# Four weight loads of a two-block recurrent attention kernel: their order, and the queue that issues them

## The chip, the cores and the metric

The kernel runs on one core of a Trainium2 chip. Its time is the device time of one execution in microseconds (us). The kernel before was run 11 times; the median counts.

## The reference

Four blocks follow each other on 2048 tokens of width 512: A, B, A, B. Each adds its output to a residual stream and works on a layer norm of it. Both A blocks share their weights, and so do both B blocks.

Block A is attention with a recurrent memory: 64 segments of 32 tokens, each behind 8 memory rows, with 32 heads of width 128. The first 8 output rows of a segment are the memory of the next, so that the segments form a chain:

```
for s in range(n_seg):
    h = jnp.concatenate([mem, xs], axis=1)
    q, k, v = h @ Wq, h @ Wk, h @ Wv          # 512 x (32 heads x 128)
    p = softmax(where(mask, q k^T * scale, -1e9))
    o = (p v) @ Wo
    mem = o[:, :M, :]; outs.append(o[:, M:, :])
```

Block B is linear attention over all tokens, 32 heads of width 16, with the weights wqkv and wo.

## The kernel before, in words

All weights of block A stay on the chip: `Wq_sb`, `Wk_sb`, `Wv_sb` and `Wo_sb`, 4 MB each. They are loaded once, at the start. The three projections of a block of 32 rows are matmuls at line 785 (`project`); each projection is made in two halves of 16 matmuls of 512 columns. Line 999 (`out_proj`) multiplies by Wo and needs all four parts of it. Line 1024 (`next_mem`) turns the new memory rows for the next segment.

Queries and keys are turned after projection (`turned`), either on TensorE (line 807) or by a DMA transpose issued from SyncE (line 798). "Left" blocks hold the last 8 tokens of four segments together; line 835 makes their scores. Line 876 makes the scores of a segment. Line 735 (`warm`) is 14 matmuls without use for the result, behind the first segment's memory attention.

The order on every engine is fixed at build time. Each piece of work is a node added with an estimated cost and, for transfers, an estimated latency `lat`; `schedule` deals the nodes out to engines by simulating these estimates. A node with a place (`P.at(step, name)`) gets the priority step x 13.5 plus an entry of the table `OFFSET`, lowest first among those that are ready (line 254). A node without a place gets the length of the path behind it. Then `finalize` turns dependences into waits on semaphores. The device executes each engine's list in order.

The loads: two come from SyncE, the first memory rows (line 644) and the first 128 tokens (line 646). Wq, Wk and Wv come from ScalarE (line 651). The offset of "ld4", -27049.20, places Wv ahead of Wq. Their estimated latencies are 13.2, 23.7 and 34.8. Wo is loaded in four parts of 1 MB from SyncE (line 656); parts 0 and 1 wait for Wk, parts 2 and 3 for Wv, by `after`. The load of block B's wqkv (line 658) follows on SyncE, and waits for the last part of Wo. Block B's wo is loaded by GpSimd (line 663) and waits for wqkv.

Of the kernel before, what the change touches and what calls it, by code (L numbers as in the profile page):

```python
# [22 lines left out]

PERIOD = 13.5
OFFSET = {
    "ld0": (-123.05,),
    "ld1": (-42.20,),
    "ld2": (6.75,),
    "ld3": (-61.40,),
    "ld4": (-27049.20,),  # L30
    "startF": (31.55,),
    "prepF": (60.65, -70.40, -52.45, 13.25, -87.60, -51.75, -71.05, 30.70, -58.30, 4.70, -58.20),
    "left0F": (-67.40, -16.05, 42.40, -9.10, 43.45, -14.00, -72.75, 13.95, -5.65, 15.60, -9.65, -120.75, 45.95,
# [103 lines left out]
class _Prog:  # L137
# [27 lines left out]
    def add(self, engs, fn, cost, reads=(), writes=(), tiles=(), dsem=None, urgent=False, mode="full",  # L165
            after=(), lat=0.0):
        nd = _Node()
        nd.mode = mode
        nd.lat = lat
        nd.key = None  # L170
        if self.place is not None:
            step, name = self.place
            nd.key = (step, name, self.count)
            self.count += 1
        nd.soft = set()
        nd.engs = (engs,) if isinstance(engs, str) else tuple(engs)
        nd.cost = cost if isinstance(cost, dict) else {e: cost for e in nd.engs}
        nd.fn = fn
        nd.sync = set(after)
        nd.order = set()  # L180
        nd.tiles = tuple(tiles)
        nd.dsem = dsem
        nd.urgent = urgent
        nd.eng = nd.start = nd.done = nd.know = None
        nd.sig = False
        nd.val = 0
        nd.waits = []
        nd.idx = len(self.nodes)
        if dsem is not None:
            self.dma_tot[dsem] = self.dma_tot.get(dsem, 0) + 16  # L190
            nd.dval = self.dma_tot[dsem]
        for key in reads:
            st = self.res.setdefault(key, [None, []])
            if st[0] is not None:
                nd.sync.add(st[0])
            st[1].append(nd)
        for key in writes:
            st = self.res.setdefault(key, [None, []])
            if st[0] is not None and st[0] is not nd:
                nd.sync.add(st[0])  # L200
            for r in st[1]:
                if r is not nd:
                    nd.sync.add(r)
            st[0] = nd
            st[1] = []
        for tl in nd.tiles:
            if tl.ops:
                p = tl.ops[-1]
                if p.engs == ("pe",) and nd.engs == ("pe",):
                    nd.order.add(p)  # L210
                else:
                    nd.sync.add(p)
            tl.ops.append(nd)
        self.nodes.append(nd)
        return nd
# [270 lines left out]
def bass_interleave_layers__memory_aug_recurrent_mem_tr__linear_attn_block__prompt_kernel(  # L486
    nc: bass.Bass,
    A_x: bass.AP,
    A_mem0: bass.AP,
    A_Wq: bass.AP,  # L490
    A_Wk: bass.AP,
    A_Wv: bass.AP,
    A_Wo: bass.AP,
    A_seg_len: bass.AP,
    B_x: bass.AP,
    B_wqkv: bass.AP,
    B_wo: bass.AP,
    out: bass.AP,
):
    _build_kernel(nc, A_x, A_mem0, A_Wq, A_Wk, A_Wv, A_Wo, A_seg_len, B_wqkv, B_wo, out)  # L500


def _build_kernel(nc, A_x, A_mem0, A_Wq, A_Wk, A_Wv, A_Wo, A_seg_len, B_wqkv, B_wo, out):
# [23 lines left out]
    def sb(name, shape, dt=BF16):  # L527
        return E(nc.sbuf_tensor(name, shape, dt))
# [4 lines left out]
    Wo_sb = sb("Wo_sb", [128, H, D])  # L533
# [78 lines left out]
    P = _Prog(nc, banks)  # L612
    add = P.add
# [33 lines left out]
    late = []  # L647
# [4 lines left out]
    wo_view = A_Wo.rearrange("h e d -> e h d")  # L652
    P.at()
    for i in range(4):
        hs = slice(8 * i, 8 * i + 8)
        add("sp", lambda s, hs=hs: s.dma_start(Wo_sb[:, hs, :], wo_view[:, hs, :]), 0.9, writes=[("Wo", i)],
                 dsem="dWo%d" % i, after=[late[1 + i // 2]], lat=(12.5, 14.5, 7.3, 9.8)[i])
    add("sp", lambda s: s.dma_start(wqkv_sb[:, :, :], B_wqkv.rearrange("(c p) f -> p c f", p=128)), 0.5,
        writes=["wqkv"], dsem="dwqkv", after=[P.nodes[-1]], lat=5.0)
    late.append(P.nodes[-1])  # L660
# [37 lines left out]
    for j in range(4):  # L698
        q = slice(32 * j, 32 * j + 32)
        d = j % 2  # L700
# [8 lines left out]
        writes=["selz"])  # L709
# [10 lines left out]
    def _m0(t, tl=tl):  # L720
        for c in range(4):
# [4 lines left out]
         writes=["memT0"])  # L726
# [610 lines left out]
```

## Time and profile before

| | |
|---|---|
| time, median of 11 runs | 1808.25 us (1803.25 to 1812.69) |
| time of the profiled execution | 1807.0 us |
| its span, from first to last instruction | 1804.8 us |
| TensorE matmuls busy | 1678.2 us, 93% |
| ScalarE busy | 1166.2 us, 65% |
| VectorE busy | 954.1 us, 53% |
| GpSimd busy | 326.0 us, 18% |
| granted TensorE clock, mean | 0.994 |
| time to landing of Wv, Wq, Wk, from issue | 13.7, 23.2, 33.7 us |
| time to landing of a part of Wo | 5.8 to 8.9 us, median 7.1 |

The profile is of one execution. In its lines PE is TensorE, PEld its weight loads, DVE VectorE, ACT ScalarE, POOL GpSimd, SP SyncE; a q behind the name means the engine's queue of instructions that issue or wait. L785 is line 785 of the kernel. `arena_sb` is one large buffer that holds nearly all working tiles, so a DMA from `arena_sb` to `arena_sb` is a transpose of line 798. A line of waits names who waited, for whom, how long in total, how often, and the longest.

### The profile page before, as it was taken

The numbers are of one execution on the slowest core, as the hardware profiler recorded it, in microseconds if no ns is written. First come the engines' busy times: TensorE is split into PE (matmuls) and PEld (weight loads), VectorE is DVE, ScalarE is ACT, GpSimd is POOL, SyncE is SP. The second block draws the span as 40 slices with busy tenths as digits, with TensorE's granted clock in tenths as the row PEclk, the third lists the DMA queues.
The fourth block names the chain that finished last, engine by engine and source line by source line (L and its number), as shares of the span: only waits on it lengthen the run. The fifth ranks groups of instructions, "written<-read, shape, count | busy, mean of one in ns | idle before, by whom it ended". The sixth has DMA issues, their size and how long they took to land.

```text
span 1804.8 us, 104738 instructions
## 1 busy us (share of the span) xinstructions
PE 1678.2 (93%) x48282; PEld 1141.6 (63%) x48407; DVE 954.1 (53%) x3216; ACT 1166.2 (65%) x3109; POOL 326.0 (18%) x660
## 2 busy tenths in 40 slices
PE   3899999999999999999789999999999999999996
PEld 1566666666666676676556666667666666666673
DVE  2355555555545555555544555555555555545557
ACT  2566666666666666666556677666666666667665
POOL 2012111211211121121101112222112222211211
PEclk9999999999999999999989999999999999999999
DMA  8412222222222222122111222212222212222223
GB/s 340 119 36 44 41 44 47 42 44 44 42 44 44 47 41 47 41 43 47 28 23 33 45 49 44 50 41 48 47 43 50 44 42 50 44 48 43 54 52 124
DMA packets 235080, 99.29 MB, mean 55 GB/s; under 512 B 213624, under 2 KB 228784, under 8 KB 233104
## 3 DMA queue, kind: packets, MB, share of 16 engines
q1 hardware_dynamic: 211312, 60.22, 17.6%
q0 software_dynamic: 21744, 19.78, 4.9%
q10 hardware_dynamic: 1584, 12.58, 1.7%
q8 instruction: 379, 6.21, 1.5%
q14 instruction: 61, 0.50, 0.1%
HBM read 29.63 MB, written 10.49 MB: 22 GB/s over the span
## 4 chain that ended last, share of the span: by engine, by line
PE 73%; DMA 15%; DVE 5%; ACT 3%; issue 2%; POOL 1%; ACTq 0%; DVEq 0%
PE pb L785 37%; PE pb L999 13%; DMA arena_sb<-arena_sb 12%; PE pb L971 4%; PE pb L876 3%; PE pb L1161 2%; PE pb L903 2%; PE pb L807 2%; DMA Wk_sb<-in_A_Wk_dram 2%; PE pb L1195 1%; DVE arena_sb L619 1%; ACT arena_sb L618 1%; PE pb L948 1%; PE pb L1024 1%; PE pb L917 1%
## 5 line engine op out<-in xcount | busy, mean ns | idle before, releaser
L618 ACT ACTIVATE arena_sb<-pb 128x512 bf16<-128x512 f32 (+5 forms) x1387 | 705.5, 511 | 333.9 <-PE pb L785 278.0
L634 POOL DMA_DIRECT2D dx_sb<-y_sb x504 | 253.2, 509 | 872.0 <-DVE y_sb L1035 494.9
L785 PE MATMUL pb<-Wv_sb,arena_sb 128*32 128x512 bf16 x5120 | 380.7, 380 | 0.0
L619 DVE COPY arena_sb<-pb 128x512 bf16<-128x512 bf16 (+2 forms) x365 | 131.3, 361 | 396.7 <-PE pb L807 382.4
L785 PE MATMUL pb<-Wq_sb,arena_sb 128*32 128x512 bf16 x5120 | 321.4, 382 | 10.2 <-DMA Wq_sb<-in_A_Wq_dram 9.8
L785 PE MATMUL pb<-Wk_sb,arena_sb 128*32 128x512 bf16 x5120 | 321.4, 381 | 3.8 <-DMA Wk_sb<-in_A_Wk_dram 2.7
L999 PE MATMUL pb<-Wo_sb,arena_sb 128*32 128x256 bf16 x10368 | 315.9, 273 | 6.1 <-DVE arena_sb L920 5.2
L999 PEld LDWEIGHTS pb<-Wo_sb,arena_sb 128*32 128x32 bf16 x10368 | 263.6, 97 | 28.8 <-DVE arena_sb L920 16.2
L785 PEld LDWEIGHTS pb<-Wq_sb,arena_sb 128*32 128x32 bf16 x5120 | 144.4, 97 | 129.8 <-DMA Wq_sb<-in_A_Wq_dram 10.1
L785 PEld LDWEIGHTS pb<-Wk_sb,arena_sb 128*32 128x32 bf16 x5120 | 136.5, 97 | 118.3 <-DVE arena_sb L619 10.2
L619 DVE CAST arena_sb<-pb 128x512 bf16<-128x512 f32 (+3 forms) x346 | 164.7, 477 | 71.6 <-PE pb L785 37.7
L619 DVE COPY arena_sb<-arena_sb 32x320 bf16<-32x320 bf16 (+1 forms) x677 | 150.1, 222 | 86.8 <-PE pb L876 68.4
L618 ACT ACTIVATE outW_sb<-pb 128x128 fp32r<-128x128 f32 x323 | 89.5, 277 | 123.0 <-PE pb L999 117.5
L876 PEld LDWEIGHTS pb<-arena_sb 128*32 128x32 bf16 x8128 | 109.4, 94 | 91.1 <-DMA arena_sb<-arena_sb 43.4
L876 PE MATMUL pb<-arena_sb 128*32 128x8 bf16 x8128 | 132.1, 174 | 35.2 <-DMA arena_sb<-arena_sb 30.6
L785 PEld LDWEIGHTS pb<-Wv_sb,arena_sb 128*32 128x32 bf16 x5120 | 122.7, 95 | 54.7 <-issue 1.5
L971 PE MATMUL pb<-arena_sb 128*128 128x128 bf16 x1024 | 145.1, 218 | 5.5 <-issue 2.7
L887 ACT ACTIVATE arena_sb<-pb 128x192 bf16<-128x192 f32 (+1 forms) x256 | 83.8, 328 | 97.8 <-PE pb L876 96.7
L972 PE MATMUL pb<-arena_sb 128*128 128x32 bf16 x1024 | 127.3, 178 | 0.0
L1035 DVE TENSOR_TENSOR y_sb<-pb,outW_sb 64x256 bf16<-64x256 f32 x158 | 65.8, 417 | 98.4 <-ACT outW_sb L618 95.0
L807 PEld LDWEIGHTS pb<-id_sb,arena_sb 128*32 128x32 bf16 x4352 | 84.5, 96 | 44.5 <-issue 8.1
L894 DVE TENSOR_TENSOR arena_sb<-arena_sb 128x128 bf16<-128x128 bf16 x504 | 90.0, 220 | 39.2 <-ACT arena_sb L887 38.3
(116 smaller groups left out, 2102.2 us busy)
## 6 DMA issues: line engine op xcount, KB each, us to landing
arena_sb<-arena_sb SPq DMA_TRANSPOSE x368, 2.8
Wv_sb<-in_A_Wv_dram ACTq DMA_DIRECT2D x1, 4096.0 KB, 13.7
Wq_sb<-in_A_Wq_dram ACTq DMA_DIRECT2D x1, 4096.0 KB, 23.2
Wk_sb<-in_A_Wk_dram ACTq DMA_DIRECT2D x1, 4096.0 KB, 33.7
Wo_sb<-in_A_Wo_dram SPq DMA_DIRECT2D x4, 1024.0 KB, 7.1
xs_scratch<-x_sb POOLq DMA_DIRECT2D x32, 128.0 KB, 2.1
pq_scratch<-arena_sb POOLq DMA_DIRECT2D x32, 128.0 KB, 2.0
dx_sb<-y_sb POOLq DMA_DIRECT2D x252, 12.0 KB, 2.0
```

Of the source, the lines that this page charges most:

```text
L618: return e.activation(o() if callable(o) else o, i() if callable(i) else i, ACTF.Copy)
L619: return e.tensor_copy(o() if callable(o) else o, i() if callable(i) else i)
L634: add(eng, lambda e: e.dma_start(o, i), 0.55 if eng == "pool" else 0.4, reads=reads, writes=writes, dsem="%s%d" % (kind, k), lat=lat + (0. ...
L785: r = pe.matmul(tl.f32()[32 * j:32 * j + 32, 0:512], blk[:, c, :], W[:, c, o:o + 512], start=(c == 0), stop=(c == 3), tile_position=(0, 32 ...
L807: r = pe.transpose(tt.bf16()[32 * j:32 * j + 32, 128 * i:128 * i + 128], img[:, k, o:o + 32], id_sb[:, :], tile_position=(0, 32 * j))
L876: r = pe.matmul(tl.f32()[32 * j:32 * j + 32, 48 * i + o:48 * i + o + n], kk[:, hh, j, :], qT[:, hh, j, 0:n], start=True, stop=True, tile_p ...
L887: add("act", lambda a: a.activation(PQ[:, r2, b, :, 0:nq], tl.f32()[:, 0:192].rearrange("p (i q) -> p i q", i=4)[:, :, 0:nq], ACTF.Exp, sc ...
L894: add("dve", lambda v, a=a: v.tensor_tensor(Pm[:, k, a, :].rearrange("p (i j x) -> p i j x", i=4, j=4), PQ[:, r2, b, :, 40 * a:40 * a + 8] ...
L971: pe.matmul(o, vimg[:, r2, e], Pbx[:, hh, :, 0:32], start=True, stop=False)
L972: return pe.matmul(o[:, :, 24:32], vleft[:, g2, e], Pbx[:, hh, :, 32:40], start=False, stop=True)
L999: r = pe.matmul(tl.f32()[32 * j:32 * j + 32, 0:256], oT[:, 4 * hh + n, :], Wo_sb[:, 8 * n + hh, 256 * d:256 * d + 256], start=(hh == 0 and ...
L1035: add("dve", lambda v: v.tensor_tensor(y_sb[0:64, k, :], tl.f32()[0:64, 0:256], outW[64:128, w, :].bitcast(F32), ALU.add), c_dve(256), rea ...
```

## The change

Queries, keys, values: the five offsets of the single loads become zero, so ScalarE issues Wq, Wk and Wv in this order. The four parts of Wo move from SyncE to ScalarE and follow there without a wait. The planner's estimates for Wo change with it: an issue cost of 0.5 in place of 0.9, and latencies of 36.5 to 44.6 from the issue. SyncE keeps the two first loads, the transposes and wqkv. Nothing else differs in the source; the planner deals the whole program out again.

```diff
 OFFSET = {
-    "ld0": (-123.05,),
-    "ld1": (-42.20,),
-    "ld2": (6.75,),
-    "ld3": (-61.40,),
-    "ld4": (-27049.20,),
+    "ld5": (0.00, 10.00, 20.00, 30.00),
+    "ld0": (0.00,),
+    "ld1": (0.00,),
+    "ld2": (0.00,),
+    "ld3": (0.00,),
+    "ld4": (0.00,),
...
     P.at()
     for i in range(4):
         hs = slice(8 * i, 8 * i + 8)
-        add("sp", lambda s, hs=hs: s.dma_start(Wo_sb[:, hs, :], wo_view[:, hs, :]), 0.9, writes=[("Wo", i)],
-                 dsem="dWo%d" % i, after=[late[1 + i // 2]], lat=(12.5, 14.5, 7.3, 9.8)[i])
+        P.at(-6000, "ld5")
+        P.count = i
+        add("act", lambda a, hs=hs: a.dma_start(Wo_sb[:, hs, :], wo_view[:, hs, :]), 0.5, writes=[("Wo", i)],
+            dsem="dWo%d" % i, lat=36.5 + 2.7 * i)
+    P.at()
     add("sp", lambda s: s.dma_start(wqkv_sb[:, :, :], B_wqkv.rearrange("(c p) f -> p c f", p=128)), 0.5,
         writes=["wqkv"], dsem="dwqkv", after=[P.nodes[-1]], lat=5.0)
```

## The prediction

> **What bounds the kernel now.** I read the page first, then the chain of waits, then what TensorE waited for in the first 60 us and after it, then the queues of ScalarE and SyncE in order of time, then stretches. TensorE is busy 93% of the span, but not evenly (stretches; columns: us, then busy us of TensorE, its weight loads, VectorE, ScalarE, GpSimd, then clock, DMA share, GB/s):
> ```profile
> 0.00:60.00 60.00, 30.27 (x632) 16.46 (x636) 15.70 (x43) 17.96 (x48) 10.69 (x45) 0.97 0.86 311
> 60.00:850.00 790.00, 755.27 (x22346) 520.75 (x22382) 422.08 (x1461) 519.73 (x1400) 142.84 (x279) 1.00 0.24 44
> ```
> Half of the first 60 us is idle; afterwards TensorE works 96% of the time. The chain that ended last says how it starts:
> ```profile
> 1.83 33.74 DMA Wk_sb<-in_A_Wk_dram
> 35.57 0.04 issue
> 35.62 4.45 PE pb L785 x48
> ...
> 52.88 5.58 DMA arena_sb<-arena_sb
> 58.46 0.14 issue
> 58.60 0.28 PE pb L835 x16
> 58.87 0.87 PE pb L785 x16
> 59.74 1.77 PE pb L999 x64
> ```
> The key weights' landing at 35.57 starts it; from there to the first output projection (L999) is 59.74 - 35.57 = 24.2 us. Of TensorE's waits in these 60 us (total, times, longest) I show those that come after the first weights could be used; the 10.6 us at L760 above them pass before 14 us, while tokens and weights are still on their way:
> ```profile
> PE pb L785 <- DMA Wq_sb<-in_A_Wq_dram: 9.8, 1, 9.8
> PE pb L785 <- DMA Wk_sb<-in_A_Wk_dram: 2.7, 1, 2.7
> ...
> PE pb L835 <- issue: 1.9, 1, 1.9
> PE pb L835 <- DMA arena_sb<-arena_sb: 1.6, 1, 1.6
> ```
> The loads leave ScalarE as values, queries, keys, one behind the other, while TensorE uses them as queries, keys, values: the first use of Wv stands at 49.6, 35 us after it landed (0.80 + 13.7 = 14.5). Wo leaves SyncE in two pairs:
> ```profile
> 0.80 0.42 ACTq L651 DMA_DIRECT2D Wv_sb<-in_A_Wv_dram  x1
> 1.25 0.55 ACTq L651 DMA_DIRECT2D Wq_sb<-in_A_Wq_dram  x1
> 1.83 0.53 ACTq L651 DMA_DIRECT2D Wk_sb<-in_A_Wk_dram  x1
> 2.39 1.28 ACT L666 ACT_TABLE_LOAD   x1 [2.39 <-issue]
> ```
> ```profile
> 35.59 1.02 SPq L656 DMA_DIRECT2D Wo_sb<-in_A_Wo_dram  x2
> 43.42 4.83 SPq L798 DMA_TRANSPOSE arena_sb<-arena_sb  x2
> 48.30 1.21 SPq L656 DMA_DIRECT2D Wo_sb<-in_A_Wo_dram  x2
> 52.88 1.19 SPq L798 DMA_TRANSPOSE arena_sb<-arena_sb  x1
> ```
> The second pair waits for Wv, long there, but stands behind two transposes that need key work, so it leaves at 48.30 and lands at about 57 (5.8 to 8.9 us to landing). The DMA engines fall idle meanwhile (share 0.00 at 47 to 48 us).
>
> **What the Trainium skill says.** "DMA: Bandwidth & Descriptors", section "Issuing engines are not separate DMA queues": whichever engine issues a transfer, it runs on the same 16 DMA engines. So moving Wo to ScalarE adds no bandwidth; it takes away waits. The same page, "Queues, rings and completion order": an engine of the DMA works through one queue's ring in order and alternates between queues packet by packet. The trace agrees: three loads of one queue land at 14.5, 24.45 and 35.57, one after the other, and a transpose of SyncE's queue beside bulk traffic took 5.58 us against a median of 2.5 in the first 110 us. "TensorE: Matmul & The Clock Gate", Part 1: the array starts at half clock after an idle window of about 3.4 us. Here the stretch 36 to 39 us shows clock 0.50, after a gap of 2.7 us.
>
> **The change, part by part.**
> *Order of three loads.* Each is 4.19 MB and they follow each other at about 10 us. Queries land at 14.5 instead of 24.45, keys at 24.45 instead of 35.57 (11.1 us sooner), values at about 35.5 instead of 14.5. Query work took 24.51 to 32.95, 8.4 us, so it now ends at 22.9 and TensorE waits some 1.5 us for the keys. ScalarE's copies for the first token block end at 14.02, just before.
> *From keys to the first L999.* The same instructions take 23.9 us (35.62 to 59.56, its first start), stalls of 1.9 and 1.6 and the half clock included: 24.45 + 23.9 = 48.4. The values are first used at 49.6 - 11.1 = 38.5, 3 us after they land: hidden. Without that cover, each us late is one us.
> *Wo in the same queue.* Four more issues on ScalarE, at 0.42 to 0.55 each (L651; 0.40 to 0.59 on SyncE): about 2.0 us. Behind them stand the table load (2.39 to 3.67) and two small copies, which end at 4.1 and now at 6.1; the next work of ScalarE is at 10.90, behind the token load, so this is hidden with 4.8 us over. SyncE loses four issues (2.2 us) and two waits, so its transposes are no longer queued behind Wo.
> *When Wo lands.* Its rows are 1 KB. In the stretches 39 to 43 us the first pair moved at 384, 355, 355, 368 GB/s; 4.19 MB at 365 is 11.5 us. Data of the third weight fell off at about 33.5; four transposes now lie in this time. SyncE's queue took 17.6% of 1804.8 us for 368 transposes and some other loads, so at most 0.86 each: 3.5 us. Last comes landing after data, 1 to 2 us (Wk: 33.5 against 35.57). 33.5 + 3.5 + 11.5 + 1.5 = 50.0. All four parts are needed by the first L999, so Wo ends 1.6 us after TensorE's own 48.4 and sets it: 59.6 becomes 50.0, **9.6 us sooner**. Bounds: 48.4 with transposes that take little (11 us gain); 53 with transposes slowed and Wo at the 325 GB/s of 51 to 52 us (6.5 us gain).
> *What follows.* The wqkv load still waits for Wo's last part, then GpSimd's load of the second Wo: they move along (54.29 and 62.63 become about 50 and 58). The next transposes, 4.9 us after L999, meet them as they did before (4.17 us to landing at 64.47); I take 0.6 us for a worse meeting, from none to 1.4 (5.58 - 4.17). Nothing later hangs on a fixed time. The work after is bound by TensorE, so the head start should reach the end: 9.6 - 0.6 = **9.0 us**.
> *The order by the planner.* It deals all instructions out by its own figures, and these change a little, which I follow for order only. By the code, it takes queries to land at 14.1, keys 25.0, values 35.3, last Wo 46.96; now 13.7, 24.6, 36.1, 47.56. Thus it had already planned for queries, keys, values, and the order on TensorE should hardly alter: shifts of -0.4 to +0.8, and after the first L999 all work hangs on that one chain. I cost a different order at nothing, within -3 to +20 us.
>
> Sum on the profiled execution: span 1804.8 - 9.0 = 1795.8; its time is 1807.0 (2.2 us lie around the span), so 1798.0. The median, 1808.25, stands 1.25 above that execution: 1799.3.
>
> **The rivals.**
> *Eaten by new waits (no change).* Transposes at about 23 and 33 us now meet rows of 8 KB instead of 1 KB, alternating by packet. For: 5.58 us even beside small rows, and 1.9 us of unexplained issue at 43.65 with the DMA engines full, which may repeat. Against: those transposes are needed only at 45 to 47 us. It would take three stalls of about 3 us: 1808.
> *The planner deals otherwise (slower).* Place: the waits of TensorE on transposes, 30.6 us in 48 waits after 60 us, and idle in steady stretches of 4%. With 127 segments after the first, 0.15 us more in each is 19 us, less 9.0 is +10: 1818. It decides from 9.0 / 127 = 0.07 us a segment. For: shifts of 0.4 to 0.8 us that aren't equal let ready times cross, and priorities fitted one by one needn't suit another order. Against: the planned landings differ so little.
> *ScalarE held by its own queue (slower).* Wo adds 4096 rows of 1 KB to 1536 of 8 KB outstanding; if the queue can't hold them, ScalarE stands still at the issue. Held until t instead of 10.90, query work starts 3.6 later, then 8.4 and 23.9: first L999 at t + 36. It loses from t = 24; held until Wv is in (35), 1820. Against: no issue shown took over 0.59 us, though no more than three loads were ever queued here.
>
> **How the numbers follow.** A measurement tells this kernel from no change beyond about 0.2% (3.6 us). Head start carried: 0.57, its own range 1796 to 1802.5 (gain 12 to 6). Partly carried, 1802.5 to 1804.6: 0.04. Eaten: 0.13, 1804.6 to 1811.9. Planner: 0.20, mostly 1812 to 1828. ScalarE held: 0.06, 1812 to 1822. So faster 0.61, same 0.13, slower 0.26. The range for 8 in 10 leaves out little below and 0.15 above: 1795 to 1821.
>
> **What would show it.** Right: TensorE's wait for Wq nearly gone, one of 1 to 2 us for Wk, first L999 at 50 and released by Wo's landing, the last L999 (1767.8 at most now) some 9 us sooner, stretches after it still at 96%. Wrong in a step: a ScalarE issue of several us; a wait of L785 on Wv; L835 waiting on transposes for longer than 1.6; the first L999 early but the distance from it to the end longer than 1804.8 - 59.6 = 1745.2, which would be the planner.

## The result and the profile after

The changed kernel takes 1820.51 us (median of 13 runs, 1817.17 to 1825.91), measured beside the kernel before at 1808.88 us. The ratio is 1.0065, with a 95% interval of 1.0052 to 1.0077: 11.8 us slower (9.4 to 13.9). The forecast was 9.0 us faster. In the changed kernel the line numbers have moved by 4 or less: L999 is L1003, L785 is L789, L807 is L811, L666 is L670, L656 is L659, L750 is L754, L754 is L758, L760 is L764.

ScalarE's queue in order of time (start, duration, engine, line, what; in brackets the idle time before it):
```profile
0.81 0.42 ACTq L652 DMA_DIRECT2D Wq_sb<-in_A_Wq_dram  x1
1.26 0.54 ACTq L652 DMA_DIRECT2D Wk_sb<-in_A_Wk_dram  x1
1.83 0.53 ACTq L652 DMA_DIRECT2D Wv_sb<-in_A_Wv_dram  x1
2.39 34.92 ACTq L659 DMA_DIRECT2D Wo_sb<-in_A_Wo_dram  x4
37.34 1.28 ACT L670 ACT_TABLE_LOAD   x1 [37.34 <-issue]
38.64 0.29 ACT L754 ACTIVATE st_sb<-st_sb,epsb_sb 128x1 f32<-128x1 f32 x1
```
The four issues of Wo took 34.92 us in all, where the prediction gave them 2.0. ScalarE stood in them until 37.3. Behind them waited the table load and the first layer norm's L754, which is 27.7 us later than the same instruction before (38.64 against 10.90):
```profile
10.90 0.29 ACT L750 ACTIVATE st_sb<-st_sb,epsb_sb 128x1 f32<-128x1 f32 x1 [6.76 <-DVE st_sb L749]
```
The chain that ended last now starts in those issues, one after the other:
```profile
2.39 8.61 ACTq L659
11.03 19.23 ACTq L659
30.29 4.06 ACTq L659
34.38 2.94 ACTq L659
...
39.67 0.62 PE pb L764 x4
...
70.74 1.95 PE pb L1003 x64
```
The weights themselves had landed as forecast: Wq at 14.4, Wk at 24.4, Wv at 34.3, the last part of Wo at 46.3. TensorE did not wait for them. Of its waits in the first 60 us (total, times, longest) only one is longer than 3.1 us in all, the one for the layer norm that ScalarE could not finish:
```profile
PE pb L764 <- DVE arena_sb L758: 37.8, 2, 36.3
```
This wait was 10.6 us before, so 27.2 us came in. Gone are the waits for Wq (9.8) and Wk (2.7) and those of the left tokens' scores (1.9 and 1.6, L835 before), 16.0 us together. That leaves 11.2 us, smaller waits apart, and the first output projection starts at 70.74 instead of 59.56, 11.2 us later. In the long stretch after it TensorE is as busy as before (us, then busy us of TensorE first; 755.27 before):
```profile
60.00:850.00 790.00, 756.19 (x22202) 518.07 (x22242) 420.06 (x1452) 517.34 (x1391) 139.70 (x273) 1.00 0.24 45
```
From the first output projection to the end of the profiled execution it is 1750.3 us, against 1745.2 before. The prediction had named a longer distance as the mark of a worse order from the planner. But the profiled execution took 2.7 us more than its kernel's median and the one before 1.9 us less than its own (1808.88), so that of the 5.1 us some 0.5 are left.

### The profile page after: what moved, and what is told of

Read it like the earlier page. It is cut to its first block, busy times and chain, and to the rows that moved or that the text cites. A ratio compares the mean times of both kernels' runs of the same rounds, so it can differ in the third digit from the quotient of the medians.

```text
span 1821.0 us, 104737 instructions
## 1 busy us (share of the span) xinstructions
PE 1679.5 (92%) x48282; PEld 1139.4 (63%) x48407; DVE 955.4 (52%) x3219; ACT 1165.4 (64%) x3106; POOL 325.8 (18%) x660
## 4 chain that ended last, share of the span: by engine, by line
PE 73%; DMA 12%; DVE 5%; ACT 4%; issue 3%; ACTq 2%; POOL 1%; DVEq 0%
PE pb L789 37%; PE pb L1003 13%; DMA arena_sb<-arena_sb 11%; PE pb L975 4%; PE pb L880 3%; PE pb L1165 3%; PE pb L907 2%; PE pb L811 2%; ACTq L659 2%; PE pb L1199 2%; ACT arena_sb L619 1%; DVE arena_sb L620 1%; PE pb L952 1%; PE pb L1028 1%; PE pb L921 1%
## 5 line engine op out<-in xcount | busy, mean ns | idle before, releaser
L789 PE MATMUL pb<-Wv_sb,arena_sb 128*32 128x512 bf16 x5120 | 380.0, 380 | 0.0
L1003 PE MATMUL pb<-Wo_sb,arena_sb 128*32 128x256 bf16 x10368 | 316.7, 273 | 6.7 <-DVE arena_sb L924 5.6
L789 PE MATMUL pb<-Wq_sb,arena_sb 128*32 128x512 bf16 x5120 | 320.7, 381 | 0.3 <-DVE arena_sb L620 0.3
L789 PE MATMUL pb<-Wk_sb,arena_sb 128*32 128x512 bf16 x5120 | 319.6, 380 | 0.8 <-DVE arena_sb L620 0.5
L1003 PEld LDWEIGHTS pb<-Wo_sb,arena_sb 128*32 128x32 bf16 x10368 | 264.1, 97 | 29.4 <-DVE arena_sb L924 16.4
L789 PEld LDWEIGHTS pb<-Wq_sb,arena_sb 128*32 128x32 bf16 x5120 | 142.7, 97 | 121.6 <-issue 2.9
L789 PEld LDWEIGHTS pb<-Wk_sb,arena_sb 128*32 128x32 bf16 x5120 | 134.9, 97 | 114.8 <-DVE arena_sb L620 10.4
L789 PEld LDWEIGHTS pb<-Wv_sb,arena_sb 128*32 128x32 bf16 x5120 | 121.2, 95 | 55.6 <-issue 1.3
L811 PEld LDWEIGHTS pb<-id_sb,arena_sb 128*32 128x32 bf16 x4352 | 84.1, 96 | 46.0 <-issue 8.2
## 6 DMA issues: line engine op xcount, KB each, us to landing
Wq_sb<-in_A_Wq_dram ACTq DMA_DIRECT2D x1, 4096.0 KB, 13.6
```

Source lines behind the costliest of these rows:

```text
L789: r = pe.matmul(tl.f32()[32 * j:32 * j + 32, 0:512], blk[:, c, :], W[:, c, o:o + 512], start=(c == 0), stop=(c == 3), tile_position=(0, 32 ...
L811: r = pe.transpose(tt.bf16()[32 * j:32 * j + 32, 128 * i:128 * i + 128], img[:, k, o:o + 32], id_sb[:, :], tile_position=(0, 32 * j))
L1003: r = pe.matmul(tl.f32()[32 * j:32 * j + 32, 0:256], oT[:, 4 * hh + n, :], Wo_sb[:, 8 * n + hh, 256 * d:256 * d + 256], start=(hh == 0 and ...
```

## The experiments

Lines of a kernel below are its own: in those that start from the changed kernel they are as above, and where an edit adds lines, later ones move with it (the table load is L666 before, L670 or L673 below). Two theories at first. H: ScalarE is held at the issue of Wo because its queue takes no more, and everything behind in its order is late. Rival O: the order of the loads, or the planner's other order that comes with it, costs the time. After the first four runs theory T joined them: a DMA transpose that runs beside loads of 8 KB rows takes the head start away even where ScalarE is not held. The expectations in us were set with the kernel before at 1808.88; beside the runs below it took 1803.29 to 1804.72, so the ratios are what is compared.

**The order alone.** The five offsets become zero as in the change; Wo stays as it was on SyncE.
```diff
-    "ld2": (6.75,),
...
-    "ld4": (-27049.20,),
+    "ld2": (0.00,),
...
+    "ld4": (0.00,),
```


> One part of the change alone: queries, keys, values in this order on ScalarE; Wo stays on SyncE with its waits. Theory H (ScalarE is held at the issue of Wo because its queue has no room, and all its later work starts late): nothing is held, ScalarE's table load starts at 2.4 us, the first L750 at about 11, the first L999 at 48 to 53, time 1797 to 1804. Rival O (the order queries, keys, values, or the planner's other order that comes with it, is what costs): slower than before, 1815 to 1821.

Measured: 1803.91 beside 1803.29 us, ratio 0.9997 (0.9985 to 1.0009), and the first L999 at 56.6, where H had 48 to 53. No loss, so O falls; but none of the forecast gain either. ScalarE was free from 2.4 us and the keys were in at 25.6, yet it stood still later. ScalarE's queue, and under it three pieces of the chain that ended last:
```profile
21.80 0.60 ACT L618 ACTIVATE arena_sb<-pb 128x512 bf16<-128x512 f32 x1 [1.38 <-PE pb L785]
36.75 1.57 ACT L618 ACTIVATE arena_sb<-pb 128x512 bf16<-128x512 f32 x3 [14.35 <-DMA arena_sb<-arena_sb]
```
```profile
22.42 14.25 DMA arena_sb<-arena_sb
36.75 1.09 ACT arena_sb L618 x2
...
56.62 1.95 PE pb L999 x64
```
The transpose issued at 22.42 landed 14.25 us later. ScalarE's next copy, of the fourth projection of the left tokens, writes the buffer that this transpose reads: `img` has two places for left blocks (`NIL = 2`), and queries and keys take turns, so that all four query projections use the same one. The copies of the keys stand behind it in ScalarE's order. That is where most of the head start went. The 3.0 us that were left of it at the first L999 can't be seen in the time.

**Wo on ScalarE alone.** The change's other part, with the old offsets, so that values come first.
```diff
-        add("sp", lambda s, hs=hs: s.dma_start(Wo_sb[:, hs, :], wo_view[:, hs, :]), 0.9, ...
+        add("act", lambda a, hs=hs: a.dma_start(Wo_sb[:, hs, :], wo_view[:, hs, :]), 0.5, ...
```


> The other part alone: Wo's four parts behind the three loads in ScalarE's queue without waits, but values still first. H: the same rows stand in the same queue, so the fourth issue of Wo ends at about 37 us again, the first L750 at 38.6, the first L999 at about 70.5, time 1818 to 1823. Rival O: 1806 to 1811, as before.

Measured: 1815.96 beside 1803.29, ratio 1.0071 (1.0058 to 1.0084); the first L754 at 38.70, the first output projection at 68.5. ScalarE's queue:
```profile
2.39 34.98 ACTq L659 DMA_DIRECT2D Wo_sb<-in_A_Wo_dram  x4
37.40 1.28 ACT L670 ACT_TABLE_LOAD   x1 [37.40 <-issue]
```
This part alone makes the whole loss.

**A hold without Wo.** The kernel before, its orders and loads untouched, with one wait put in front of the table load.
```diff
+            if nd.eng == "act" and nd.dsem is None and not cnt.get("held"):
+                cnt["held"] = 1
+                waits.append((sidx["dWk"], 16))
             nd.waits = waits
```


> The kernel before, every instruction in its old order, loads as they were; only ScalarE's table load now waits until Wk has landed (35.6 us). It leaves Wo on SyncE. H: a hold of ScalarE alone makes the loss: the first L750 at about 37, the first L999 at 68 to 70, 9 to 10 us later than the 59.6 of before, time 1816 to 1820. Rival O, or a loss that comes from Wo's transfer beside other traffic: less than 3 us slower than before.

Measured: 1815.24 beside 1803.29, ratio 1.0074 (1.0058 to 1.0090); the first output projection at 72.3, some 2 us later than expected; TensorE waited 3.4 us for a transpose on the way. ScalarE's queue shows the hold, and the chain that ended last its end:
```profile
34.28 1.28 ACT L670 ACT_TABLE_LOAD   x1 [34.28 <-DMA Wk_sb<-in_A_Wk_dram]
```
```profile
63.95 7.22 DMA arena_sb<-arena_sb
...
72.45 3.37 PE pb L1003 x64
```
A hold of ScalarE of this length is enough for the loss, with no row of Wo in its queue.

**Wo from GpSimd.** The changed kernel's orders, with the four issues moved after planning to GpSimd, behind its setup.
```diff
     P.schedule()
+    wo = [n for n in P.committed if n.dsem and n.dsem.startswith("dWo") and ...]
+    rest = [n for n in P.committed if n not in wo]
+    pl = [i for i, n in enumerate(rest) if n.eng == "pool"]
+    at = pl[40] + 1
+    for n in wo:
+        n.eng = "pool"
+    P.committed = rest[:at] + wo + rest[at:]
```


> The changed kernel with every engine's order kept, except that Wo's four issues stand in GpSimd's queue behind its setup (at about 15 us), where nothing else is due until wqkv has landed. H: ScalarE goes on at 2.4 us, the first L999 at 48 to 52 (Wo lands at about 47, or TensorE's own work ends at 48.4), time 1797 to 1802. Rival O: still 1815 or more, since all orders but that issue are the changed kernel's. Rival B (the bandwidth that four loads take from each other): Wq or Wk land over 3 us later than 14.5 and 24.5, time above 1803.

Measured: 1809.95 beside 1803.29, ratio 1.0032 (1.0019 to 1.0045); the first output projection at 64.3. Against the changed kernel it is earlier by 6.4 us with the same orders, so the hold did cost. But it misses H's 48 to 52, and the marks of rival B came: with two queues of loads at work Wk landed at 28.9 and Wv at 45.3. The chain, though, does not wait for Wk; it waits for the transpose, which fared worse still:
```profile
22.53 22.47 DMA arena_sb<-arena_sb
...
64.35 1.95 PE pb L1003 x64
```

**The transposes taken away.** The order alone (the first run above), with the second group's four left projections turned on TensorE, as the first group's are, and placed by the first group's offsets (those of the names that end in F).
```diff
-                at(step, "left%d" % b)
+                early = first and step == 2; P.at(base + step, "left%d" % b + ("F" if step < 0 or early else ""))
...
-                turned(Wq_sb, ..., False, step > 0)
+                turned(Wq_sb, ..., False, step > 0 and not early)
...                                                                  # the same for Wk_sb
```


> The order queries, keys, values with Wo on SyncE behind its waits, as before, and one thing more: the four projections of the second group of left tokens, which are turned by DMA transposes while the loads run, are turned on TensorE (four more groups of 16 small matmuls, about 0.45 us each). Theory T (without the hold it is the transpose beside 8 KB rows that eats the head start: issued at 22.42, it landed 14.25 us later, and ScalarE could not write its buffer again before): with it gone, keys start at about 25, the first L999 at 48 to 52, and the time is 8 to 10 us below the kernel before, ratio 0.9945 to 0.996. Rival C (an early first L999 does not reach the end, something later takes it back): first L999 at 48 to 52 but ratio 0.999 or more. Rival W (Wo or Wv is the limit, not the transposes): first L999 at 55 or later.

Measured: 1789.93 beside 1804.72, ratio 0.9918 (0.9893 to 0.9943): 14.8 us faster than the kernel before (10.3 to 19.3), and by the two ratios some 26 us faster than the changed one. Pieces of its chain:
```profile
26.00 2.59 PE pb L785 x48
...
47.83 1.70 PE pb L999 x54
49.54 2.52 issue
52.06 0.52 PE pb L999 x10
```
Key work at 26.0 runs on without a transpose in its way, and the first L999 comes at 47.8, where the prediction had TensorE's own work end (48.4). T holds; rivals C and W fall. Two things don't fit. Inside this first L999 TensorE stood still for 2.5 us, so the step behind it, L1024, comes only 8.9 us earlier than before. And the time fell by more than expected (ratio 0.9945 to 0.996) and by more than the start moved; the last section comes back to this.

**The same turn with the old order of loads.**
```diff
+# the two edits above, in the kernel before
```


> The kernel before with the same four projections turned on TensorE, its loads in the old order (values, queries, keys). T: there the keys at 35.6 us set the start, so little is won: the first L999 at 57 to 60, ratio 0.998 to 1.000. If the turn on TensorE alone were worth the gain: first L999 below 55, ratio below 0.997.

Measured: 1796.38 beside 1804.72, ratio 0.9959 (0.9947 to 0.9971). From its chain:
```profile
54.95 1.96 PE pb L999 x64
```
I had expected 57 to 60 and a ratio of 0.998 or more; both marks of the other reading came, that the turn alone is worth a gain. With no transposes ahead of it, Wo's second pair no longer waits on SyncE for key work (its issues end at 41.9 instead of 49.5). So at the first L999 the turn alone is worth 4.6 us, the order alone 3.0, both together 11.8; at L1024 behind it 4.6, 2.9 and 8.9. In the time it is 7.4 us, nothing that can be seen, and 14.8. Both together give more than the sum, as they should if each takes away what hides the other's gain; but half of the gain of 14.8 us comes with the turn alone.

**The change with the turn.** All of the change, hold included.
```diff
+# the two edits above, in the changed kernel
```


> The changed kernel (Wo in ScalarE's queue) with the second group's four left projections turned on TensorE. H: ScalarE is still held to about 37 us, after the loads of 8 KB rows, where a transpose landed in 2.5 us anyway; so the first L999 stays at 66 to 70 and the kernel stays 0.2% to 0.6% slower than the kernel before. If the transposes were the changed kernel's own trouble: first L999 below 60 and no slower than before.

Measured: 1813.60 beside 1804.37, ratio 1.0051 (1.0034 to 1.0069); the table load at 37.36, the first output projection 3 us later than expected:
```profile
73.25 1.96 PE pb L1003 x64
```
In the changed kernel it is the hold, not the transposes, that binds.

**The same orders, Wo first on SyncE.** As above; the four issues moved after planning to SyncE, behind the two small first loads, without waits.
```diff
...
+    pl = [i for i, n in enumerate(rest) if n.eng == "sp"]
+    at = pl[1] + 1
+    for n in wo:
+        n.eng = "sp"
```


> As the run above in every engine's order, except that Wo's four issues stand in SyncE's queue, behind the two small first loads, without waits. SyncE may be held by them for 30 us or more, but has nothing due until the transposes of the second segment at about 55 us. H (a hold costs what is queued behind it): ScalarE's table load at 2.4 us, first L999 at 48 to 53, ratio to before 0.991 to 0.996. Rival B (bandwidth: Wo's rows go between those of Wq and Wk from the start): Wq lands over 2 us later than 14.5, Wk over 4 us later than 24.5, first L999 at 53 or later.

Measured: 1795.72 beside 1804.37, ratio 0.9949 (0.9930 to 0.9969). SyncE's and ScalarE's queues, and a piece of the chain:
```profile
1.69 36.40 SPq L659 DMA_DIRECT2D Wo_sb<-in_A_Wo_dram  x4
```
```profile
2.39 1.28 ACT L670 ACT_TABLE_LOAD   x1 [2.39 <-issue]
```
```profile
49.54 1.96 PE pb L1003 x64
```
SyncE is held for 36.40 us, longer than ScalarE was, and nothing waits for it, since nothing is due there before 47. The first output projection starts at 49.5. Between this run and the one above only the engine that issues Wo differs, and with it the queue that Wo stands in: 23.7 us at the first output projection, about 18 us in the time by the two ratios. Wk landed at 27.8, 3.4 us late, so the bandwidth rival is there too, but small.

**What fills the queue.** Two profiles of the kernel before with its three loads cut up, to show the issues and not the time: twelve transfers of whole 8 KB rows, then six of half rows.
```diff
-            a.dma_start(W[:, :, :], v)
+            a.dma_start(W[:, c, :], v[:, c, :])                                # c in 0..3
```


> The kernel before, each of the three loads issued as four transfers of whole 8 KB rows (twelve transfers, the same 1536 rows, no other edit). Theory D (the queue holds a number of rows, about 135 for each of 16 DMA engines by the four holds seen): 96 rows and 12 completions for each engine fit, no issue takes over 1 us, the table load starts by 9 us. Rival N (the queue holds a number of transfers, three to six): an issue of several us from the fourth to the seventh on, table load after 11 us.


```diff
-            a.dma_start(W[:, :, :], v)
+            a.dma_start(W[:, :, 2048*c:2048*c+2048], v[:, :, 2048*c:2048*c+2048])  # c in 0..1
```


> The kernel before, each of the three loads issued as two transfers of half rows (six transfers, 3072 rows of 4 KB, the same bytes). Theory D: 192 rows and 6 completions for each engine are too many, so the fifth issue is held to about 7 us and the sixth to about 12 us, and the table load follows it. Rival N: no more held than the twelve transfers are.

ScalarE's queue with twelve transfers, and then with six:
```profile
5.00 4.81 ACTq L653 DMA_DIRECT2D Wk_sb<-in_A_Wk_dram  x4
9.84 1.28 ACT L673 ACT_TABLE_LOAD   x1 [9.84 <-issue]
```
```profile
1.83 4.74 ACTq L653 DMA_DIRECT2D Wq_sb<-in_A_Wq_dram  x2
6.60 9.97 ACTq L653 DMA_DIRECT2D Wk_sb<-in_A_Wk_dram  x2
16.60 1.28 ACT L673 ACT_TABLE_LOAD   x1 [16.60 <-issue]
```
Twice the rows in half the transfers hold ScalarE to 16.6 instead of 9.8, so rows count and a small number of transfers is not the limit, nor are the bytes, which are the same: N falls. But D's number falls as well. With twelve transfers the eleventh and twelfth issue took 1.62 and 2.17 us, with six the fourth was held already, for 4.18. The traces list every row that the queue moved, so what still stood before each of the 16 DMA engines when an issue was let go can be counted (rows, and one completion for each transfer; queued less moved): at the last issue 108 - 21 = 87 with twelve transfers and 198 - 81 = 117 with six; in the changed kernel 164 - 23 = 141 at the first issue of Wo and 359 - 179 = 180 at the last. It is no single number of rows; what exactly is counted stays open.

## Why the prediction was wrong, by its steps

*Order of three loads*: the landings were right. Forecast 14.5, 24.45, 35.5; measured 14.4, 24.4, 34.3. The work that was to follow them waited for ScalarE.

*Wo in the same queue*: this is the step that failed. "Four more issues on ScalarE, at 0.42 to 0.55 each: about 2.0 us", hidden with 4.8 us over. The price came from rows in which the queue had room (three transfers on ScalarE, pairs on SyncE), and was carried to a queue with 5,632 rows. They took 34.92 us, and the layer norm came 27.7 us late; the waits that fell away behind it covered some 16 us of this, and 11.2 us were left. The rival "ScalarE held by its own queue" had the mechanism, the place and the price (held until Wv is in: 1820), at a chance of 0.06. Its argument against, that no issue shown took over 0.59 us, was no evidence for a fuller queue. Its formula, first L999 36 us after the first layer norm, gives 74.6 for 38.64; measured 70.7. The 23.9 us in it hold stalls of 1.9 and 1.6 us and the half clock, and none of these came again (the clock was 1.00 up to 60 us, and the transposes landed in 2.4 to 2.5 us). So it is partly luck that its 1820 meets the measured 1820.5: ScalarE came 3.6 us later than its 35, and the way from there was 3.9 us shorter.

*When Wo lands*: 50.0 forecast, 46.3 measured. Its rows moved at 344 to 358 GB/s from 34 to 45 us, with no transpose beside them.

*What follows*: the head start was to reach the end, and in the changed kernel a late start did: 11.2 us at the first output projection, 11.8 (9.4 to 13.9) in the time. Over all the runs the two agree to some 4 us only (last section).

*The order by the planner*: right as far as the runs show. In the traces TensorE's order differs from the one before in a few places up to 59 us and after that, as far as can be told, only by records that one trace lacks; GpSimd's is the same, and ScalarE's differs up to 60 us only. In the run with Wo from GpSimd every other order is the changed kernel's, and its loss, 5.8 us (3.4 to 8.1), goes with its late start, 4.7. So the planner rival, given 0.20, has no visible part.

*Eaten by new waits*: I had put the transposes' lateness aside because their results are "needed only at 45 to 47". Their results are; but the buffer that they read is needed again at 22.4. The order alone shows it: 14.25 us to landing, and no gain. The rival of this name, given 0.13, had this cause and this outcome. So the forecast gain of 9.0 us was out of reach even without the hold. With both obstacles gone the first L999 is at 47.8 (Wo as before) or 49.5 (Wo without waits on SyncE), against the working's 48.4 and 50.0: to that point its sum was right for a kernel that has neither. The gains of 14.8 and 9.2 us do not confirm the 9.0, since some 4.5 us of each arise at another place (last section).

## What to carry to other kernels

An issue of a transfer is cheap only while the queue has room (here 0.4 to 0.7 us, and up to 23.3 us where there was none): price it by what already stands there in rows, and place it on an engine that has nothing due until the queue has drained. A transfer queued without a wait is not a transfer without a wait; the engine itself waits, with all its later work. And for a transpose beside bulk loads ask two things, when its result is needed and when its source is written again.

## What the runs showed of the hardware

A transpose of SyncE's queue landed in 2.4 to 2.9 us with the DMA engines nearly free, in 5.6 to 8.0 beside rows of 1 to 3 KB, in 14.25 beside rows of 8 KB in one other queue, and in 22.5 with two other queues. The Trainium skill, "DMA: Bandwidth & Descriptors", section "Queues, rings and completion order", has the DMA engines alternate between queues by packet. The packets in the traces agree, in stretches of 4 us:

| what stood in the queues | 8 KB rows | the others |
|---|---|---|
| the three loads alone (kernel before, 28 to 32 us) | 205 | |
| and a transpose (order alone, 28 to 32 us) | 195 | 197 of 256 B |
| and Wo from SyncE (Wo first on SyncE, 18 to 22 us) | 178 | 178 of 1 KB |
| and Wo from GpSimd and a transpose (28 to 32 us) | 128 | 127 of 4 KB, 129 of 256 B |

One packet of each queue goes for one of every other, whatever its size. The transpose is 512 packets, 32 for each of the 16 DMA engines, and each of these waits for a row of 8 KB; its first packet came 3.8 us after the issue. From GpSimd the same 1 KB rows of Wo went in packets of 4 KB, and the loads beside them came later (Wv at 45.3, against 39.5 with Wo on SyncE).

One difference stays open. In three of the four kernels with the turn on TensorE the time fell by about 3 to 4 us more, against the kernel before, than the first output projection moved: 7.4 for 4.6, 14.8 for 11.8, and a loss of 9.2 for 13.6; in the fourth the gain was 9.2 for 10.1. In two kernels without the turn it is the other way: no gain for a start 3.0 us earlier, and a loss of 12.8 for 8.9. The intervals are 2 to 5 us wide to each side, but a part of it has a place. From the last L1024 of the first A block to the sixth of the second it is 122.1 us before and 119.7 to 122.6 in the other kernels without the turn, but 116.7 to 117.7 in all four with it. There TensorE's waits for transposes (3.1 us between 860 and 1000 us before) are gone in all four. The edit concerns the first block's early work alone, but the planner deals all later work out again with it; which of the two reaches so far was not tested.
